# Inverting the first chunk's 32x32 blocks on TensorE instead of on VectorE, in a fused DeltaNet and SwiGLU kernel

## The chip, the cores and the metric

One core of one Trainium2 chip. The metric is the device time of one execution in microseconds (us). Stretches and waits are read from the one profiled execution of each kernel; that of the kernel before took 882.93 us. In the profile PE is TensorE, PEld its weight loads, DVE VectorE, ACT ScalarE, POOL GpSimd.

## The reference

Two stages, all in float32; the FFN weights arrive as 64-bit floats and are narrowed on the chip.

```python
# q, k, v: (4, 8, 768, 48); beta: (4, 8, 768)
k_n = k / (np.linalg.norm(k, axis=-1, keepdims=True) + 1e-06)
for t in range(S):
    kt, vt, bt = (k_n[:, :, t], v[:, :, t], beta[:, :, t, None])
    y[:, :, t] = np.einsum('bhd,bhde->bhe', q[:, :, t], state)
    v_old = np.einsum('bhde,bhd->bhe', state, kt)
    state = state + bt[:, :, :, None] * np.einsum('bhd,bhe->bhde', kt, vt - v_old)
# y is reshaped to 3072 tokens of 384; then, with rms-normed tokens xn:
g = xn @ w_gate                          # 384 x 1536
silu = g * (1.0 / (1.0 + np.exp(-g)))
return silu * (xn @ w_val) @ w_out       # 1536 x 384
```

## The kernel before

It cuts the 768 time steps into six chunks of 128. Chunk c of batch element b (eight heads) is a "unit"; there are 24. Inside a chunk the loop over t becomes matrix products, once the inverse of a unit lower triangular 128x128 matrix per head is known. The kernel inverts only its four 32x32 diagonal blocks and gets the rest by products ("corner"). FFN tiles take two units (256 tokens) each, so a chunk feeds two FFN tiles.

For each chunk all 128 blocks (4 per head, 8 heads, 4 batch elements) are sent through DRAM (`gd`) so that each block lies on one partition (`gblk`), and 31 steps of substitution with two vector instructions each turn the identity into the inverses (`ttb`). They return through DRAM (`td`) to the layout of the products (`tt`). `ne` is the same, scaled by minus beta.

```python
    def invert(c, dt):
        nc.gpsimd.memset(ttb, 0.0)
        nc.gpsimd.memset(ttb.rearrange("p j i -> p (j i)")[:, 0 : W * W : W + 1], 1.0)
        yield dt
        for i in range(W - 1):
            # ... shapes ...
            nc.vector.scalar_tensor_tensor(
                out=tmp,
                in0=gblk[:, i, None, i + 1 :].to_broadcast(shape),
                scalar=nbeta[:, c, i : i + 1],
                in1=ttb[:, 0 : i + 1, i : i + 1].to_broadcast(shape),
                op0=ALU.mult, op1=ALU.mult,
            )
            to = ttb[:, 0 : i + 1, i + 1 :]
            nc.vector.tensor_tensor(out=to, in0=to, in1=tmp, op=ALU.add)
            yield dt
        if c == 0:
            stay_warm(13, ttb[:, 0:4].rearrange("p k j -> p (k j)"))
        td = dram.tile([128, W, W], FP32, name="td")
        nc.sync.dma_start(out=td, in_=ttb)
        # ... for c > 0 the same with -beta into nd; then 16 transfers td -> tt
```

`stay_warm(n)` issues n matmuls nobody reads, to keep TensorE's clock up. The FFN weights come in tiles of 768 columns, and five vector instructions convert each; `convert(n)` places n of these steps in order by hand, and `convert_rest` deals the others out over time.

```python
        if c == 0:                       # in recur(), units 0 and 1 of chunk 0
            corner(0, None)
            corner(1, None)
            convert(1)
            stay_warm(2)
            corner(None, 0)
            # ... inner, outer, with convert() and stay_warm() between ...
            transpose_y(1, scale(*ys.pop(1)))
            convert(4)
            yield                        # from here on the FFN runs beside it
            # ... units 2 and 3 ...
```

All that follows is interleaved by a plan: a list of generators, each with a start time in steps, and each `yield dt` puts its generator dt steps later. One step is a group of FFN matmuls. The plan fixes the order in which each engine meets its instructions on the chip.

```python
    CYC = 3 * FT * B // 2
    first = recur(0, 1.2)
    # ...
    at(0, convert_rest(0.6))
    at(1, first)
    for c in range(1, NCH):
        t0 = CYC * c
        for b in range(B):
            at((8 if c == 1 else t0 - 76) + 4.5 * b, prepare(B * c + b))
        at(35 if c == 1 else t0 - 49, invert(c, 0.62))
        at(*((57, recur(c, 0.7)) if c == 1 else (t0 - 25, recur(c, 1.2))))
```

## Time and profile before

| what | value |
|---|---|
| time, median of 3 runs | 876.22 us (876.17 to 877.04) |
| profiled execution | 881.2 us |
| first FFN matmul (p_gv) | 89.8 us |
| chunk 0's FFN done (equal point, worked out in the prediction) | 233 us |
| from there to the end | 648 us |

The page of the kernel before cuts its span into 40 slices of 22 us. Each digit is a busy share in tenths; PEclk is the granted TensorE clock in tenths of full speed:

```profile
PE   6428789898999999999999999999999999999998
DVE  7594758986253491333491333491343491221100
PEclk9556889999999999999999999999999999999999
DMA  7722625402231103122103122113121113000000
```

The first four slices are the prologue. The "4" and "2" of PE, second and third, stand above the "5" and "9" of DVE: TensorE waits while VectorE substitutes, and its clock drops to 5. From the eleventh slice on PE is full. The rows of the page's table of groups for the two things that the change exchanges (line, engine, operation, tiles, shapes, count; then busy us, mean ns of one; then the idle time before them):

```profile
L443 DVE SCALAR_TENSOR_TENSOR tmp<-gblk,nbeta,ttb 128x31 f32<-128x31 f32 (+15 forms) x186 | 74.7, 402 | 13.9 <-DMA gblk<-gd 8.2
L452 DVE TENSOR_TENSOR ttb<-ttb,tmp 128x31 f32<-128x31 f32 (+15 forms) x186 | 63.6, 342 | 6.4
L793 PE MATMUL p_gv<-xt,wg_sb 128*128 128x256 f32 x864 | 218.3, 388 | 0.6 <-DVE xt L764 0.6
```

186 is six chunks of 31 steps, so a chunk's substitution costs (74.7 + 63.6)/6 = 23 us of VectorE. Only chunk 0's is exposed, since nothing else can run then.

### The profile page before, as it was taken

The numbers are of one execution on the slowest core, as the hardware profiler recorded it, in microseconds if no ns is written. First come the engines' busy times: TensorE is split into PE (matmuls) and PEld (weight loads), VectorE is DVE, ScalarE is ACT, GpSimd is POOL, SyncE is SP. The second block draws the span as 40 slices with busy tenths as digits, with TensorE's granted clock in tenths as the row PEclk, the third lists the DMA queues.
The fourth block names the chain that finished last, engine by engine and source line by source line (L and its number), as shares of the span: only waits on it lengthen the run. The fifth ranks groups of instructions, "written<-read, shape, count | busy, mean of one in ns | idle before, by whom it ended". The sixth has DMA issues, their size and how long they took to land.

```text
span 881.2 us, 20181 instructions
## 1 busy us (share of the span) xinstructions
PE 820.0 (93%) x8608; PEld 636.0 (72%) x8608; DVE 410.2 (47%) x1032; ACT 253.6 (29%) x651; POOL 95.3 (11%) x125
## 2 busy tenths in 40 slices
PE   6428789898999999999999999999999999999998
PEld 5327567676787777787777787777777777777776
DVE  7594758986253491333491333491343491221100
ACT  5503335511434312234212234212234212220101
POOL 3001132300041000131000131000130000000000
PEclk9556889999999999999999999999999999999999
DMA  7722625402231103122103122113121113000000
GB/s 187 184 72 51 181 82 157 130 5 84 48 74 34 42 19 85 38 65 39 37 34 69 38 65 40 36 42 61 38 56 22 37 43 61 2 19 1 19 0 19
DMA packets 147849, 51.05 MB, mean 58 GB/s; under 512 B 140176, under 2 KB 143248, under 8 KB 147760
## 3 DMA queue, kind: packets, MB, share of 16 engines
q1 hardware_dynamic: 123840, 35.34, 17.1%
q0 software_dynamic: 1872, 10.22, 3.5%
q10 hardware_dynamic: 22048, 4.20, 2.4%
q8 instruction: 68, 1.11, 0.5%
q14 instruction: 21, 0.17, 0.1%
HBM read 36.11 MB, written 13.63 MB: 56 GB/s over the span
## 4 chain that ended last, share of the span: by engine, by line
PE 78%; DVE 14%; DMA 2%; issue 2%; SPq 1%; ACT 1%; POOL 1%; ACTq 0%; DVEq 0%; POOLq 0%
PE p_gv L793 38%; PE p_o L780 19%; DVE tmp L443 5%; DVE ttb L452 5%; PE p_g L329 3%; PE p_y L567 2%; PE p_z L623 2%; PE p_k L605 2%; PE p_t L313 2%; PE p_y L605 2%; PE p_v L511 2%; PE p_x L641 2%; PE p_w L518 1%; PE p_z L632 1%; DVE h_f L804 1%
## 5 line engine op out<-in xcount | busy, mean ns | idle before, releaser
L780 PE MATMUL p_o<-wo_sb,h_f 128*128 128x384 f32 x576 | 217.5, 502 | 9.9 <-DVE h_f L804 9.8
L793 PE MATMUL p_gv<-xt,wg_sb 128*128 128x256 f32 x864 | 218.3, 388 | 0.6 <-DVE xt L764 0.6
L793 PE MATMUL p_gv<-xt,wv_sb 128*128 128x256 f32 x864 | 215.8, 386 | 0.0
L793 PEld LDWEIGHTS p_gv<-xt,wg_sb 128*128 128x128 f32 x864 | 161.6, 193 | 40.8 <-issue 1.7
L793 PEld LDWEIGHTS p_gv<-xt,wv_sb 128*128 128x128 f32 x864 | 161.5, 191 | 24.8 <-issue 2.5
L804 DVE TENSOR_TENSOR h_f<-sil,p_gv 128x256 f32<-128x256 f32 x144 | 60.2, 418 | 248.3 <-ACT sil L802 248.1
L802 ACT ACTIVATE sil<-p_gv 128x256 f32<-128x256 f32 x144 | 55.2, 383 | 332.0 <-PE p_gv L793 305.8
L780 PEld LDWEIGHTS p_o<-wo_sb,h_f 128*128 128x128 f32 x576 | 105.2, 192 | 62.8 <-DVE h_f L804 15.1
L443 DVE SCALAR_TENSOR_TENSOR tmp<-gblk,nbeta,ttb 128x31 f32<-128x31 f32 (+15 forms) x186 | 74.7, 402 | 13.9 <-DMA gblk<-gd 8.2
L452 DVE TENSOR_TENSOR ttb<-ttb,tmp 128x31 f32<-128x31 f32 (+15 forms) x186 | 63.6, 342 | 6.4
L343 DVE TENSOR_TENSOR gp<-p_g,mask 64x128 f32<-64x128 f32 (+1 forms) x160 | 37.6, 276 | 35.2 <-ACT gp L339 30.9
L293 POOL TENSOR_TENSOR knrm<-ksum,half 128x8 f32<-128x8 f32 x24 | 40.2, 1679 | 61.0 <-DVE ksum L292 60.9
L749 POOL TENSOR_SCALAR ms<-ms 128x1 f32<-128x1 f32 x24 | 6.5, 273 | 287.3 <-ACT y L741 287.0
L318 ACT COPY kqt<-p_t 128x512 f32<-128x512 f32 x48 | 28.0, 584 | 29.6 <-PE p_t L313 29.0
L548 ACT COPY vs<-p_v 32x256 f32<-32x256 f32 x48 | 17.4, 363 | 53.1 <-PE p_v L511 30.6
L623 PEld LDWEIGHTS p_z<-v_raw,tt 64*64 64x64 f32 x768 | 25.8, 142 | 9.4 <-issue 7.2
L435 POOL MEMSET ttb<- 128x1024 f32 x6 | 5.7, 955 | 240.5 <-DMA td<-ttb 189.1
L329 PE MATMUL p_g<-kqt 64*64 64x192 f32 x640 | 31.2, 330 | 0.0
L641 PE MATMUL p_x<-tt,gp 64*64 64x64 f32 x384 | 29.8, 233 | 0.1
L623 PE MATMUL p_z<-v_raw,tt 64*64 64x48 f32 x768 | 28.8, 227 | 0.0
L511 PEld LDWEIGHTS p_v<-tt,gp 32*32 32x32 f32 x768 | 17.6, 108 | 15.5 <-issue 11.1
L641 PEld LDWEIGHTS p_x<-tt,gp 64*64 64x64 f32 x384 | 26.4, 145 | 2.2 <-issue 1.6
(97 smaller groups left out, 803.7 us busy)
## 6 DMA issues: line engine op xcount, KB each, us to landing
kpad<-in_k_dram SPq DMA_DIRECT2D x24, 192.0 KB, 2.9
qpad<-in_q_dram SPq DMA_DIRECT2D x24, 192.0 KB, 2.7
v_raw<-in_v_dram SPq DMA_DIRECT2D x24, 192.0 KB, 3.0
raw<-in_moe_w_out_dram POOLq DMA_DIRECT2D x6, 768.0 KB, 5.0
out_dram<-o_sb SPq DMA_DIRECT2D x24, 192.0 KB, 1.9
gblk<-gd SPq DMA_DIRECT2D x6, 512.0 KB, 3.3
td<-ttb SPq DMA_DIRECT2D x6, 512.0 KB, 2.6
tt<-td SPq DMA_DIRECT2D x96, 32.0 KB, 2.2
```

Source lines behind the costliest of these rows:

```text
L293: nc.gpsimd.tensor_tensor(out=knrm, in0=ksum, in1=half, op=ALU.pow)
L329: nc.tensor.matmul(to, pair[d, K1 if i else K0], pair[d, places], skip_group_check=True)
L343: nc.vector.tensor_tensor(out=to[p, :, place], in0=p_g[p, :, place], in1=mask[p, i, None].to_broadcast([p.stop, 2, HC]), op=ALU.mult,)
L443: nc.vector.scalar_tensor_tensor(out=tmp, in0=gblk[:, i, None, i + 1 :].to_broadcast(shape), scalar=nbeta[:, c, i : i + 1], in1=ttb[:, 0 : ...
L452: nc.vector.tensor_tensor(out=to, in0=to, in1=tmp, op=ALU.add)
L605: nc.tensor.matmul(p_o[p, 2 * j : 2 * j + 2].rearrange("p h d -> p (h d)"), kq[:, j, place], st[:, j], start=(alone or j == 0), stop=alone ...
L623: nc.tensor.matmul(p_zs[b_z][p, h], tt[b_z][p, h], r[p, h], start=(h == 0), stop=(p is lo), skip_group_check=True,)
L641: nc.tensor.matmul(p_x[lo, h], gp[b_x][hi, h, HC * K0 : HC * (K0 + 1)], tt[b_x][hi, h], skip_group_check=True,)
L780: nc.tensor.matmul(p_o[i], h_f[:, i * C : (i + 1) * C], wo_sb[:, f], start=(f == f0), stop=(f == f1 - 1),)
L793: nc.tensor.matmul(p_gv[:, i], w_sb[:, t, f * 128 : (f + 1) * 128], xt[:, t], start=(t == 0), stop=(t == KT - 1),)
L802: nc.scalar.activation(out=sil, in_=p_gv[:, 0], func=ACTF.Silu)
L804: nc.vector.tensor_tensor(out=h_f, in0=sil, in1=p_gv[:, 1], op=ALU.mult)
```

## The change

The intent: get to the first FFN matmul sooner. Chunk 0's blocks are inverted where they lie, by block products on TensorE: no trip to DRAM, no 31 steps. A block is split into its eight 4x4 diagonal sub-blocks and the rest. The inner part A has A^4 = 0, so I-A has the inverse (I+A)(I+A^2); with that, the rest is some X with X^8 = 0, and I-X has the inverse (I+X)(I+X^2)(I+X^4). With the products at both ends this makes six steps of one or two rounds, each round 32 products of 32x32 blocks per unit: 320 matmuls, after 32 products of keys. Chunks 1 to 5 keep the substitution.

```diff
+    def blocks(n):
+        tiles = [(h, slice(W * a, W * (a + 1))) for h in range(H) for a in range(NBLK)]
+
+        def times(to, left, right, start=True):
+            for h, wa in tiles:
+                nc.tensor.matmul(
+                    to[wa, h],
+                    left[wa, h],
+                    right[wa, h].rearrange("p s w -> p (s w)")
+                    if len(right.shape) == 4
+                    else right[wa, h],
+                    start=start, stop=True, skip_group_check=True,
+                )
+        # ... p_d: 32 products of keys; weigh: times beta and a mask ...
+        p = ps_one()
+        plus(p, over_h(eye))
+        times(p, b_t, a_t, start=False)
+        nc.scalar.copy(a_t, p)
+        yield
+        # ... four more steps ...
+        p = ps_two()
+        times(p[:, :, 0], rx[:, :, 1], rx[:, :, 0])
+        times(p[:, :, 1], rx[:, :, 0], rx[:, :, 1])
+        # ... tt[n] and ne from p
```

The second part: a weight tile is now two k slices by 384 columns, so that the first FFN columns need three tiles instead of six, and fewer conversion steps (19 instead of 31) stand ahead of the FFN.

```diff
-WT = 768
+WT = 384
-    wg_sb = const.tile([128, KT, DFF], FP32, name="wg_sb")
-    wv_sb = const.tile([128, KT, DFF], FP32, name="wv_sb")
+    wgv_sb = const.tile([128, 2 * KT, DFF], FP32, name="wgv_sb")
...
-            raw = bits.tile([128, WT], I64, name="raw", bufs=3)
+            raw = bits.tile([128, 2, WT], I64, name="raw", bufs=3)
```

The order is new, too. `go(n)` is one step of unit n's blocks; those of units 2 and 3 partly fall behind the FFN's start (the `yield`), and all fill matmuls but the first 14 are gone:

```diff
+    def load_beta():
+        # ... four transfers into nbeta
+        nc.vector.tensor_scalar(
+            out=nbeta, in0=nbeta, scalar1=-1.0, scalar2=None, op0=ALU.mult
+        )
...
+            go(0)
+            query(1)
+            go(1)
+            transpose(3, kpad[3], K0)
             corner(0, None)
             corner(1, None)
+            go(2)
             convert(1)
-            stay_warm(2)
             corner(None, 0)
             corner(None, 1)
+            go(3)
...
             yield
+            go(3)
+            yield dt
+            go(2)
+            yield dt
+            key(2)
...
             inner(2, None, 3)
+            load_k(B)
+            load_beta()
+            mask_queries(2)
```

To make room for them, the plan sets chunk 1 and all later chunks 11 steps later (chunk 1's preparation 15). The paces of chunk 0's recurrence (1.2 to 0.8 steps) and of `convert_rest` (0.6 to 0.4) change too.

```diff
-        t0 = CYC * c
+        t0 = CYC * c + 11
-            at((8 if c == 1 else t0 - 76) + 4.5 * b, prepare(B * c + b))
-        at(35 if c == 1 else t0 - 49, invert(c, 0.62))
-        at(*((57, recur(c, 0.7)) if c == 1 else (t0 - 25, recur(c, 1.2))))
+            at((23 if c == 1 else t0 - 76) + 4.5 * b, prepare(B * c + b))
+        at(47 if c == 1 else t0 - 49, invert(c, 0.62))
+        at(*((68.5, recur(c, 0.7)) if c == 1 else (t0 - 25, recur(c, 1.2))))
```

## The prediction

> **What bounds the kernel now.** I read the page's 40 slices first, then busy time by stretches, the chain of work in the first 240 us, who PE waited for, and last the stretches around two stalls that the waits call "issue". The stretches give engine busy time, then granted TensorE clock, DMA share and GB/s:
>
> ```profile
> 0.00:240.00 240.00, 185.72 (x2356) 145.03 (x2358) 165.68 (x364) 85.10 (x194) 38.93 (x50) 0.84 0.41 107
> 240.00:860.00 620.00, 616.99 (x6196) 478.02 (x6190) 242.83 (x665) 166.04 (x451) 56.37 (x76) 1.00 0.17 40
> ```
>
> From 240 us on PE is busy 617 of 620 us at full clock: nothing but less PE work helps there, and the change takes none away. In the first 240 us, 54 us are idle and the clock averages 0.84. This is where all gain must come from. The chain there (shares of the whole span):
>
> ```profile
> by line: PE p_gv L793 18.5%; DVE tmp L443 9.5%; DVE ttb L452 8.3%; PE p_o L780 7.9%; issue 7.1%; PE p_z L623 2.4%; DMA tt<-td 2.2%; PE p_x L641 2.1%; DMA raw<-in_moe_w_gate_dram 2.0%; DMA gd<-gp 1.9%; PE p_w L518 1.9%; PE p_v L511 1.8%; PE
> ```
>
> The two DVE lines are the substitution, once for chunk 0 (about 31 to 57 us) and once for chunk 1 (180 to 210 us). In the timeline the first p_gv matmul of the FFN starts at **89.8 us**, after the blocks went out to DRAM (`gd`, landed near 31 us), 62 vector instructions, and the way back (`td`, `tt`, first use 66.6 us). From 66.6 to 89.8 us runs the recurrence of two units, half of it at clock 0.50. Waits of PE over the whole run:
>
> ```profile
> PE p_fill L183 <- DVE ttb L452: 14.2, 1, 14.2
> PE p_o L780 <- DVE h_f L804: 9.8, 7, 2.7
> PE p_g L402 <- ACT kqt L318: 8.6, 4, 2.9
> PE p_w L527 <- issue: 6.1, 2, 3.8
> ```
>
> The last row looks small and matters most for this change. The two stalls come in the only places where many 32x32 matmuls run without anything large between them:
>
> ```profile
> 66.60:68.30 1.70, 1.66 (x122) 1.52 (x123) 0.32 (x1) 0.39 (x2) 0.44 (x1) 0.51 0.64 84
> 68.30:70.60 2.30, 0.01 (x1) 0.01 (x2) 0.11 (x1) 0.34 (x1) 0.00 (x0) 0.50 0.86 315
> 99.68:100.85 1.17, 1.17 (x122) 1.17 (x121) 1.16 (x2) 0.46 (x2) 0.00 (x0) 1.00 0.92 360
> 100.85:104.86 4.01, 0.17 (x21) 0.06 (x9) 1.87 (x4) 0.36 (x1) 0.54 (x1) 0.91 0.51 110
> 104.86:115.00 10.14, 10.14 (x71) 7.74 (x71) 3.70 (x6) 3.59 (x8) 0.00 (x0) 0.53 0.18 71
> ```
>
> After some 60 matmuls (122 records: a matmul has two, and as many weight loads) PE stands still for 2.3 and 4.0 us, and after the longer one its clock is 0.53 for 10 us. The DMA view names the candidate:
>
> ```profile
> q8 instruction: 68, 1.11, 0.5%
> ```
>
> 68 packets of 16 KB are 17,408 instructions of 64 bytes; PE has 8608 matmul and 8608 weight-load records, 17,216 together. So q8 feeds PE, one packet lasts 256 instructions or **64 matmuls**, and its packets start at 67.75, 71.5 and 75.25 us, a distance of 3.75 us, with PE running again at 70.59.
>
> **What the Trainium skill says.** "Runtime: NRT & Kernel Launch", section "Instruction fetch mechanics", says that the sequencer fetches the next 16 KiB block of 256 instructions while it works on the current one, and that crossing a boundary is mostly hidden. The block size agrees with the trace; "mostly hidden" holds after 240 us and not in the two bursts above. "TensorE: Matmul & The Clock Gate", section "What's actually happening", says the clock falls to half after an idle window of about 3.4 us and rises after as much sustained work. The trace agrees roughly: 0.53 after the 4.0 us gap, 1.00 in the first 20 us with PE busy 67%, 0.61 in 20 to 30 us with PE busy 42%. "TensorEngine Tiling (Array Packing)", section "Key Properties", says that tiles work independently; with four diagonal 32x32 blocks in turn the trace has 59 matmuls in 1.17 us, 20 ns each, against 62 ns (32 in 1.98 us at clock 0.50, 16 in 0.99 at full) where only two blocks alternate.
>
> **The change, part by part.** I took instruction orders of both kernels and multiplied counts by durations of the trace before.
>
> Removed before the first FFN matmul: the 31 steps of substitution (62 DVE instructions, 23 us), `gd`, `gblk`, `td` and `tt` transfers of chunk 0, 27 of the fill matmuls, the transposes L527. The weight tiles also change: both kernels have 18 tiles of 768 columns' worth with 5 DVE steps (0.55+0.96+0.56+1.0+0.96 = 4.0 us), but the first FFN columns now need 3 tiles ready instead of 6, so 19 conversion steps stand ahead of the FFN instead of 31: about 9 us of DVE moved behind.
>
> Added per unit: 32 products p_d, 256 matmuls 32 wide and 64 matmuls 64 wide, four identity products. At 36, 20 and 30 ns and 0.42 us that is 1.2+5.1+1.9+1.7 = **9.9 us of PE**, some 40 us for four units. DVE gets about 3.6 us per unit, ACT nine copies of 0.37 or 0.59 us. With two units interleaved the six steps hide each other's copies.
>
> Start of the FFN. Summed by order, PE has 45 us of full-clock work between the first p_d (near 9.5 us) and the first p_gv. Walking the steps through PE, ACT and DVE with these durations gives the last block of units 0 and 1 near 37 us and the first p_gv at 56 us, if nothing else stands in the way. But these 45 us hold about 1220 matmuls, 1245 from the start, or 19.5 blocks of instructions. Two are there at the start; the first fetch begins at matmul 64, near 12 us; 17.5 fetches at 3.7 us (an estimate from the distance of 3.75 us above) are 65 us, so **12 + 65 = 77 us**. I take 75 (range 62 to 88): fetches are sometimes quicker than that, or hidden behind wider matmuls. Gain at this point 15 us, not the 34 that the steps alone would give.
>
> From there to the end of chunk 0's FFN. Before: 127.7 us (89.8 to 217.5) for 105 us of full-clock PE work, with four of 24 FFN column blocks (15.5 us) left; the equal point is 217.5+15.5 = 233 us. After: 136 us of PE work (93 FFN, 12 blocks of units 2 and 3, 31 scores, transposes and recurrence), since units 2 and 3 are now solved behind the FFN's start. DVE has 116 us in it. The 555 matmuls at its beginning are 29 us of work and 8.7 fetches, 32 us. With 8 to 10 us of other losses (before: 23, of which 4 the stall and some 6 the half clock) it is 148 us, and ends at 75+148 = 223 us.
>
> Then chunk 1's recurrence. The plan sets it and everything after it 11 steps later against the FFN; by the order PE has nothing of the FFN among its first 25 us of small matmuls. Before it lay among p_gv from 217.5 us and PE was 99.9% busy. I count 8 us lost to copies between the steps, less 2 for fewer switches between tile shapes: 6 us. From chunk 2 on both are the same.
>
> Sum: 233 - 223 - 6 = 4 us gained; optimistic at every estimate (start 62, middle 144) 21 us; pessimistic (88 and 155) a loss of 16. I shade the centre by some 4 us towards the optimistic side, because the start has the most doubtful estimate: **868 us**.
>
> **Rivals.** (a) Steps bind, fetch is hidden: FFN at 56 to 62 us, end 850 to 856. For it: after 240 us PE shows no such stall. Against it: there 64 matmuls take over 5 us (245 in the 20 us from 220), here some 2.2. (b) Half clock: with the fill matmuls gone and PE waiting on fetches and copies, the clock falls to 0.50 in the prologue; the small matmuls cost up to double, FFN at 80 to 88, end 875 to 885. For it: 0.50 from 30 to 60 us before. Against it: PE is then busier than 42%. (c) DVE becomes the bound behind the FFN's start, as 12 more conversion steps lie there and h_f stands behind them in order: 116 us in 148 is 78%, the same share as before (99.6 of 127.7), so I expect waits of p_o on h_f like the 9.8 us now, not a bound. (d) Uncovered recurrence of chunk 1 costs 15 us: then the time is that of before.
>
> **Range and chances.** Range 851 to 884, from the sums above with not all estimates off the same way. Faster by over 2% means under 859, a gain of 17.5 us, which needs rival (a) almost whole: 0.22. Slower by over 2% (over 894) needs (b) and (d) together: 0.05. Within 2%: 0.73.
>
> **What would show it.** The first p_gv near 75 us; PE stalls called "issue" between bursts of the block products, and packets of the instruction queue 3.5 to 4 us apart from 15 to 75 us; PE busy some 60% there. If the first p_gv comes before 64 us and those packets are 2 to 3 us apart, my fetch estimate is wrong and (a) holds. Chunk 0's FFN ending near 223 us, a stretch of some 32 us of recurrence without p_gv after it, and the same 660 us from there to the end as before would bear out the rest. A clock of 0.50 in the slices from 20 to 60 us speaks for (b).

## The result, and the profile after

The changed kernel is correct and slower. Its median is 927.69 us (926.32 to 932.21, four runs) against 876.63 us of the kernel before on the same chip (876.17 to 877.57, four runs). The ratio is **1.059** (95% interval 1.056 to 1.062). A ratio here is the mean time of one kernel's fast runs over that of the other's of the same rounds, so it is not quite the ratio of the medians quoted.

The page after:

```profile
span 930.4 us, 25271 instructions
PE   7778896889889999999999999999999999999998
DVE  6425448933923438424349133366143383121110
PEclk7877999989977999999999999999999999999999
q8 instruction: 88, 1.44, 0.6%
L511 DVE SCALAR_TENSOR_TENSOR tmp<-gblk,nbeta,ttb 128x31 f32<-128x31 f32 (+15 forms) x155 | 62.2, 401 | 10.0 <-DMA gblk<-gd 5.3
```

The substitution of chunk 0 is gone (155 = 5 x 31), and VectorE's full third slice ("9" before) is now a "2". PE is busier in the prologue than it was, and yet the prologue takes as long. There is also something new: PE's clock is at 7 in the twelfth and thirteenth slices, 256 to 302 us, where PE was at full clock before. The instruction queue q8 has 88 packets instead of 68.

Two marks cut both profiled executions into comparable stretches:

| stretch | before | after | difference | predicted |
|---|---|---|---|---|
| start to first p_gv | 89.8 | 88.7 | -1 | -15 |
| to the end of chunk 0's FFN | 143 | 172.5 | +29 | +5 |
| from there to the end | 648 | 669 | +21 | +6 |
| sum | 881 | 930 | +49 | -4 |

The sum differs by 49 us, the medians by 51. The end after is read from the last p_o matmuls of chunk 0's FFN, which finish at 261.2 us. Busy times by stretches (stretch, length, then busy time and records of PE, PEld, DVE, ACT, POOL, then granted clock, DMA share, GB/s), first of the kernel before:

```profile
10.00:89.80 79.80, 42.87 (x799) 36.21 (x799) 55.19 (x117) 29.24 (x61) 7.87 (x10) 0.66 0.45 113
89.80:233.00 143.20, 129.94 (x1349) 97.35 (x1350) 102.13 (x217) 49.49 (x121) 24.85 (x28) 0.93 0.37 102
```

and of the changed kernel:

```profile
10.00:88.70 78.70, 60.85 (x2417) 51.14 (x2415) 33.69 (x70) 28.24 (x64) 10.97 (x14) 0.72 0.25 69
88.70:261.20 172.50, 146.51 (x1978) 110.35 (x1978) 111.00 (x230) 56.73 (x137) 33.27 (x42) 0.95 0.31 88
261.20:305.80 44.60, 38.57 (x782) 35.42 (x781) 12.05 (x27) 12.57 (x32) 4.97 (x9) 0.73 0.31 62
```

In the first, PE stands idle for 18 us and is at 0.72 of its clock. In the second it is idle for 26 us, 13 more than before, and has 17 us more of work. The third is chunk 1's recurrence with no FFN matmul in it at all: chunk 0's FFN is used up, and chunk 1's needs what this recurrence makes. The longest waits of PE in the whole run:

```profile
PE p_b L557 <- issue: 15.8, 11, 2.3
PE p_o L1017 <- DVE h_f L1041: 15.6, 10, 3.1
PE p_y L718 <- DVE u L799: 5.8, 2, 5.0
```

p_b is the tile of the block products. Their timeline shows the bursts (start, length, then what ran; the bracket is the idle time before):

```profile
15.89 0.95 PE L557 MATMUL p_b<-wo_sb 32*32 32x32 f32 x51
18.52 0.42 PE L557 MATMUL p_b<-wo_sb 32*32 32x32 f32 x13 [1.67 <-issue]
```

The packets of the instruction queue start (to the half microsecond below) at 15.5, 19.5, 23.5, 27.5, 31.5, 34.5 us and so on to 86.5 us: 19 packets, 3.94 us apart on average, right up to the first p_gv.

### The profile page after: what moved, and what is told of

It reads as the page before. It is cut to its first block, busy times and chain, and to the rows that moved or that the text cites. A ratio compares the mean times of both kernels' runs of the same rounds, so it can differ in the third digit from the quotient of the medians.

```text
span 930.4 us, 25271 instructions
## 1 busy us (share of the span) xinstructions
PE 870.8 (94%) x11146; PEld 681.3 (73%) x11146; DVE 399.6 (43%) x1000; ACT 264.4 (28%) x684; POOL 108.8 (12%) x149
## 4 chain that ended last, share of the span: by engine, by line
PE 78%; DVE 13%; issue 4%; DMA 2%; ACT 1%; POOL 1%; SPq 1%; ACTq 0%; DVEq 0%; POOLq 0%
PE p_gv L1030 34%; PE p_o L1017 16%; DVE tmp L511 4%; PE p_b L557 4%; DVE ttb L520 3%; PE p_g L398 3%; PE p_t L382 2%; PE p_y L718 2%; PE p_z L774 2%; PE p_k L756 2%; PE p_x L792 2%; PE p_v L681 2%; PE p_y L756 2%; PE p_z L783 1%; PE p_w L688 1%
## 5 line engine op out<-in xcount | busy, mean ns | idle before, releaser
L1030 PE MATMUL p_gv<-xt,wgv_sb 128*128 128x256 f32 x1728 | 413.5, 386 | 0.7 <-DVE xt L1001 0.7
L1030 PEld LDWEIGHTS p_gv<-xt,wgv_sb 128*128 128x128 f32 x1728 | 322.0, 191 | 64.7 <-issue 3.7
L1017 PE MATMUL p_o<-wo_sb,h_f 128*128 128x384 f32 x576 | 217.5, 501 | 15.6 <-DVE h_f L1041 15.6
L511 DVE SCALAR_TENSOR_TENSOR tmp<-gblk,nbeta,ttb 128x31 f32<-128x31 f32 (+15 forms) x155 | 62.2, 401 | 10.0 <-DMA gblk<-gd 5.3
L520 DVE TENSOR_TENSOR ttb<-ttb,tmp 128x31 f32<-128x31 f32 (+15 forms) x155 | 53.0, 342 | 4.9
L358 POOL TENSOR_TENSOR knrm<-ksum,half 128x8 f32<-128x8 f32 x24 | 41.0, 1709 | 79.7 <-DVE ksum L357 75.1
L774 PEld LDWEIGHTS p_z<-v_raw,tt 64*64 64x64 f32 x768 | 28.3, 148 | 9.6 <-issue 6.6
L792 PE MATMUL p_x<-tt,gp 64*64 64x64 f32 x384 | 32.3, 241 | 1.8 <-ACT tt L701 1.8
L774 PE MATMUL p_z<-v_raw,tt 64*64 64x48 f32 x768 | 31.8, 235 | 1.3 <-issue 0.8
L718 PE MATMUL p_y<-u,gp 128*64 128x48 f32 x768 | 27.5, 227 | 5.8 <-DVE u L799 5.8
L718 PEld LDWEIGHTS p_y<-u,gp 128*64 128x64 f32 x768 | 26.3, 144 | 6.4 <-issue 5.3
```

The lines of the kernel that those rows point to most:

```text
L358: nc.gpsimd.tensor_tensor(out=knrm, in0=ksum, in1=half, op=ALU.pow)
L511: nc.vector.scalar_tensor_tensor(out=tmp, in0=gblk[:, i, None, i + 1 :].to_broadcast(shape), scalar=nbeta[:, c, i : i + 1], in1=ttb[:, 0 : ...
L718: nc.tensor.matmul(p_y[p, h], gp[b_y][:, h, HC * place : HC * (place + 1)], u[:, h], start=(c == 0 and h == 0), stop=True, skip_group_chec ...
L774: nc.tensor.matmul(p_zs[b_z][p, h], tt[b_z][p, h], r[p, h], start=(h == 0), stop=(p is lo), skip_group_check=True,)
L792: nc.tensor.matmul(p_x[lo, h], gp[b_x][hi, h, HC * K0 : HC * (K0 + 1)], tt[b_x][hi, h], skip_group_check=True,)
L1017: nc.tensor.matmul(p_o[i], h_f[:, i * C : (i + 1) * C], wo_sb[:, f], start=(f == f0), stop=(f == f1 - 1),)
```

## The experiments

Theory: **(1)** the prologue is bound by instruction fetch, 64 small matmuls per packet and some 4 us per packet, whatever the products cost; **(2)** the 11 steps of delay in the plan strip chunk 1's recurrence of its FFN cover, so it runs alone, at half clock; **(3)** VectorE's order (conversions and the wait for `nbeta` ahead of what the FFN needs) makes the idle time between. Rivals: the six steps' chain of copies binds the prologue and not the fetch; the weight tiles are at fault; the low clock is the cause and not a companion. The experiments ran in four calls, on chips 3 and 7, with medians of the kernel before between 879.08 and 881.47 us instead of 876.63; so they are compared by ratio to the kernel before of their own call. The changed kernel itself was not run again, so ratios that differ from its 1.059 by less than about half a per cent are not told apart. The first p_gv comes from one execution each: the change, e_plan and e_warm share one prologue and have it at 88.7, 86.8 and 88.4 us, so 2 us there mean nothing.

| run | what | ratio to before | 95% interval | first p_gv us | chunk 1's first p_v us |
|---|---|---|---|---|---|
| (before) | | 1 | | 89.8 | 217.4 |
| (the change) | | 1.059 | 1.056 to 1.062 | 88.7 | 262.6 |
| e_pair | 2 heads per block product (wrong result) | 1.030 | 1.024 to 1.036 | 75.1 | 242.5 |
| e_quad | 4 heads per block product (wrong result) | 1.026 | 1.020 to 1.032 | 62.1 | 228.3 |
| e_plan | the 11 steps undone | 1.041 | 1.036 to 1.046 | 86.8 | 247.6 |
| e_tiles | before + weight tiles | 0.996 | 0.990 to 1.001 | 86.0 | 205.6 |
| e_warm | clock kept up in chunk 1 | 1.055 | 1.050 to 1.060 | 88.4 | 263.5 |
| e_beta | `nbeta` negated later | 1.051 | 1.047 to 1.055 | 88.3 | 258.5 |
| e_qpb | quad + plan + beta (wrong result) | 1.004 | 0.998 to 1.009 | 66.8 | 216.3 |
| e_tiles2 | before + tiles, converted later | 1.003 | 0.999 to 1.008 | 86.4 | 213.7 |
| e_conv | change + 12 conversions earlier | 1.054 | 1.050 to 1.058 | 93.0 | 262.2 |
| e_pbc | plan + beta + conv | 1.035 | 1.032 to 1.038 | 90.9 | 242.3 |
| e_qpbc | quad + plan + beta + conv (wrong result) | 0.998 | 0.994 to 1.003 | 67.8 | 207.1 |
| e_tiles3b | before + tiles, converted earlier | 0.989 | 0.985 to 0.993 | 90.7 | 207.6 |

### Fewer, wider block products: e_pair and e_quad

One matmul takes the columns of two (or four) heads, with the left block of the first. The result is wrong on purpose (relative error 0.11 and 0.14), but the steps, copies and bytes stay; only matmuls and weight loads become fewer, and each wider.

```diff
             for h, wa in tiles:
+                if h % 4:                      # 2 in e_pair
+                    continue
+                hs = slice(h, h + 4)
                 nc.tensor.matmul(
-                    to[wa, h],
+                    to[wa, hs],
                     left[wa, h],
-                    ... right[wa, h]
+                    ... right[wa, hs]
```

> The changed kernel, but each block product takes two heads in one matmul (one stationary block, 64 or 128 streamed columns instead of 32 or 64): the result is wrong on purpose, the columns streamed and the chain of steps are the same, and 640 of the 1280 block matmuls fall away, 10 instruction packets. Theory of instruction fetch: the first FFN matmul moves from 88.7 us to 65 to 75 us, the time falls by 20 to 37 us, to 890 to 907 us. Rival (the chain of steps, the array's own time, or the half clock sets the start): less than 6 us change, 921 us or more.

> The same with four heads in one matmul: 960 of 1280 block matmuls fall away, 15 packets. Fetch: the first FFN matmul at 55 to 68 us, the time 30 to 50 us below the changed kernel, 878 to 897 us, with less gained by the second halving than by the first since then the steps bind. Rival: less than 6 us change.

Measured: the first p_gv comes at 75.1 and 62.1 us instead of 88.7, with 78 and 73 instruction packets in all instead of 88. The prologue of e_quad, and the stretch behind it:

```profile
10.00:62.10 52.10, 46.61 (x1169) 34.77 (x1167) 33.38 (x70) 27.54 (x64) 10.95 (x14) 0.84 0.37 101
62.10:227.00 164.90, 144.29 (x1306) 106.19 (x1306) 111.30 (x231) 56.16 (x137) 33.64 (x42) 0.94 0.32 92
```

From 10 us to the first p_gv, PE is idle for 5.5 us instead of 17.9 and has a clock of 0.84 instead of 0.72. The chain of steps and copies is whole in this kernel, so that rival falls: the number of matmuls bound the prologue. 26.6 us came back at the first p_gv, though the waits called "issue" before it in the changed kernel sum to only 13.4 us. The rest is busy time, 46.6 us instead of 60.9. Busy time times clock is some 39 us instead of 44 (an estimate from these lines), so the rest is partly work saved (about 5 us at full clock) and partly the higher clock. The second line shows what did not come back: the way from the first p_gv to the end of chunk 0's FFN still takes 165 us.

Since fewer matmuls also mean fewer weight loads, this pair of runs cannot quite tell fetch from the array's own work. The probes below do.

### The disputed cost by itself: e_probe_n and e_probe_w

In the kernel before, PE stands idle while chunk 0 is substituted. There, 192 matmuls of 32x32 by 32 columns were put in, or 48 with 128 columns: the same columns streamed, a quarter of the instructions.

```diff
+            if i == 25:
+                for r in range(192):           # 48 in e_probe_w
+                    x = slice(W * (r % NBLK), W * (r % NBLK + 1))
+                    nc.tensor.matmul(
+                        p_fill[0][x, 0:32], ident[x, x], ident[x, 0:32], skip_group_check=True
+                    )                          # 0:128 in e_probe_w
```

> The kernel before with 192 extra 32x32 matmuls of 32 columns (four diagonal tiles in turn, fp32, result unused) in the stretch from 43 to 57 us, where PE only waits for DVE and DMA is 20% busy. Theory of instruction fetch: bursts of about 64 matmuls with pauses between, one packet of the instruction queue per burst, 3.5 to 4 us apart, 10 to 13 us in all, 55 to 65 ns each. Rival (a fixed issue cost of each small matmul): an even row without pauses, the same spacing from first to last, 20 to 35 ns each, 4 to 7 us in all.

> The same columns in 48 extra matmuls of 128 columns. Theory: less than one packet, no pause of over 1.5 us, 4 to 7 us in all. If the array's own time bound the narrow ones, both take the same time.

One look each (880.65 and 880.36 us, both correct, no interval). The added matmuls in the timeline; first the narrow ones, of which each makes two records:

```profile
42.58 1.84 PE L878 MATMUL p_fill<-ident 32*32 32x32 f32 x153
46.25 1.56 PE L878 MATMUL p_fill<-ident 32*32 32x32 f32 x128 [1.83 <-issue]
49.98 1.61 PE L878 MATMUL p_fill<-ident 32*32 32x32 f32 x103 [2.17 <-issue]
```

and the wide ones:

```profile
41.23 4.65 PE L878 MATMUL p_fill<-ident 32*32 32x128 f32 x96
```

The narrow ones run 64 matmuls (128 records) in 1.56 us and then stop until the next packet. The packets start at 43.5, 47.25 and 51.0 us: 3.75 us for 64 matmuls, of which 1.6 is work. The wide ones, with as many columns in all, run without a pause in 4.65 us and need one packet, at 42.25 us. They also load weights a quarter as often, but a burst that ends at 64 matmuls, stops, and goes on when the next packet has come is not a cost of weight loads: the pause belongs to the number of instructions. What the probes do not settle is the end of the prologue: from 60 to 80 us of the changed kernel PE is busy for 17.9 of 20 us at a clock of 0.51, and there fetch and the half clock cannot be told apart.

### The plan's 11 steps: e_plan

```diff
-        t0 = CYC * c + 11
+        t0 = CYC * c
-            at((23 if c == 1 else t0 - 76) + 4.5 * b, prepare(B * c + b))
+            at((12 if c == 1 else t0 - 76) + 4.5 * b, prepare(B * c + b))
-        at(47 if c == 1 else t0 - 49, invert(c, 0.62))
-        at(*((68.5, recur(c, 0.7)) if c == 1 else (t0 - 25, recur(c, 1.2))))
+        at(36 if c == 1 else t0 - 49, invert(c, 0.62))
+        at(*((57.5, recur(c, 0.7)) if c == 1 else (t0 - 25, recur(c, 1.2))))
```

> The changed kernel with the plan's shift of 11 steps taken back (chunk 1's preparation at 12, its inversion at 36, its recurrence at 57.5, every later chunk 11 steps earlier), so that chunk 1's recurrence lies among FFN matmuls again, as before. Theory that the uncovered recurrence costs (44.6 us for 25 us of work): the time falls by 10 to 20 us, to 908 to 918 us. Rival (PE then waits in its order for DVE's inversion of chunk 1, which is no earlier): within 5 us of 927.7 us.

Measured: 1.041, which is 1.8 points less, correct. Its stretches:

```profile
86.80:247.60 160.80, 133.57 (x1914) 100.31 (x1915) 109.56 (x225) 55.17 (x133) 35.68 (x42) 0.92 0.34 95
247.60:300.00 52.40, 49.93 (x932) 40.24 (x933) 17.63 (x43) 16.57 (x42) 10.60 (x14) 1.00 0.29 57
```

Chunk 1's recurrence, from 247.6 us, now has FFN matmuls among it: PE is busy for 49.9 of 52.4 us at a clock of 1.00, against 38.6 of 44.6 at 0.73. So (2) holds: the delay, meant to make room, cost about 15 us (1.8% of 877 us). It could be taken out without another change.

### The half clock: e_warm

Eight fill matmuls go into each of the first three steps of chunk 1's recurrence.

```diff
+            if c == 1 and s < 0:
+                p_warm = ps_delta([128, 128], "p_warm")
+                for i in range(8):
+                    nc.tensor.matmul(p_warm, ident, ident, skip_group_check=True)
```

> The changed kernel with eight 128x128 fill matmuls ahead of each of the first three steps of chunk 1's recurrence, so that PE is busy while it waits for tt from DRAM. In the changed kernel that recurrence takes 44.6 us, at clock 0.50 from 266 to 288 us, for some 25 us of work. Theory (the gaps at its start drop the clock, and the half clock costs): clock near 1.00 there, the gap between FFN matmuls of 45.5 us falls to 28 to 36 us, the time by 8 to 16 us to 912 to 920 us. Rival (its chain of copies costs): the gap stays over 40 us and the time within 3 us of 927.7 us.

The same two stretches, first of the changed kernel, then of e_warm:

```profile
270.00:275.00 5.00, 5.00 (x87) 4.52 (x86) 0.56 (x1) 1.36 (x4) 0.00 (x0) 0.50 0.49 117
275.00:280.00 5.00, 5.00 (x75) 4.58 (x75) 1.10 (x2) 1.32 (x3) 0.00 (x0) 0.50 0.23 50
```

```profile
270.00:275.00 5.00, 4.93 (x133) 4.44 (x132) 0.56 (x1) 1.72 (x5) 0.00 (x0) 1.00 0.37 57
275.00:280.00 5.00, 5.00 (x145) 4.59 (x142) 1.66 (x3) 1.83 (x5) 0.00 (x0) 1.00 0.47 123
```

The fills bring the clock to 1.00, and PE gets through 278 records instead of 162 in the same ten us. From the end of the last p_o to the next p_gv it is 44.6 us in the changed kernel (261.2 to 305.8) and 38.4 us in e_warm (262.2 to 300.6); the 45.5 us of the expectation were read with another mark. Only 16 of the 24 fills lie in this gap, the other eight ran at 229 us among the FFN. The 16 are 4.6 us of work, of which some 2 us only fill waits for `tt` (3.6 us in the changed kernel, 1.6 in e_warm). So the recurrence alone would take some 34 to 36 us at full clock, and the half clock costs some 9 to 11 us there; this is an estimate from these numbers. The fills spend a good part of what they save. In the time itself 1.055 is not told apart from 1.059.

### VectorE's order: e_beta and e_conv

e_beta moves the negation of `nbeta`, which waits for its transfer, from `load_beta` to the start of chunk 1's substitution, out of the way of `u`, which stood behind it in order. e_conv puts twelve conversion steps back ahead of the FFN.

```diff
-        nc.vector.tensor_scalar(out=nbeta, in0=nbeta, scalar1=-1.0, ...)   # load_beta
+        if c == 1:                                                         # invert
+            nc.vector.tensor_scalar(out=nbeta, in0=nbeta, scalar1=-1.0, ...)
```

```diff
-            convert(3)
+            convert(9)
...
-            convert(1)
+            convert(7)
```

> The changed kernel with the negation of nbeta moved from just behind its transfer's issue to the start of chunk 1's inversion. Theory: the wait of p_y for u of 5.0 us goes (DVE stood in order behind the transfer of nbeta), and the time falls by 4 to 7 us. Rival (DVE's conversions take the place of this wait): less than 2 us.

> The changed kernel with 12 more conversion steps ahead of the FFN, placed where its DVE is idle (37.2 to 54.9 us), so 31 as in the kernel before. Theory (12 steps, some 9.5 us of DVE, were moved behind the FFN's start although it did not come earlier, and DVE bounds the stretch from there to chunk 1's recurrence): the first FFN matmul stays at 87 to 91 us, chunk 1's recurrence starts 5 to 10 us earlier than 261.2 us, the time falls by 5 to 10 us. Rival (PE's own work and fetches bound that stretch): less than 3 us.

The wait of VectorE in the changed kernel, and what PE still waited for `u` in e_beta, where it had been 5.8 us:

```profile
DVE nbeta L237 <- DMA nbeta<-in_beta_dram: 3.9, 1, 3.9
```

```profile
PE p_y L719 <- DVE u L800: 3.2, 2, 2.5
```

The wait shrinks by 2.6 us and does not go. The profiled execution is 4.3 us shorter, but that of the change was the slowest of its runs (span 930.4 us, the others 924.5 to 926.4, against 926.1 here), so this says nothing. The ratio, 1.051, lies 0.8 points under that of the change, but on another chip, where e_warm and e_conv, too, lie 0.4 and 0.5 under it. With e_conv PE waits 9.8 us for `h_f` between its first p_gv at 93.0 us and 262 us, instead of 12.6 us; but its first p_gv comes 4.3 us later, and chunk 1 starts at 262.2 us instead of 262.6. What was won behind the FFN's start had been paid ahead of it. My expectation of a gain is not borne out. So of (3) the waits are seen in the traces; that mending them wins time is not shown.

### Together: e_qpb, e_pbc and e_qpbc

> Four heads per block matmul (wrong result on purpose), the plan's shift taken back and the negation of nbeta moved, all three together. If the three costs are separate they add: 900.8 - 11.6 - 5 = 884 us (880 to 889). If they share a cause (a later stage has to wait for chunk 1's inversion on DVE anyway), the sum is less: 890 us or more.

> The changed kernel with three parts mended, result correct: the plan's shift taken back, the negation of nbeta moved, 12 conversion steps ahead of the FFN. If they add (11.6, 5 to 6, and 5 to 10 us): 900 to 907 us. If they share the wait for chunk 1's inversion: 908 to 915 us. Above 880 us in any case, since the instruction fetch stays.

> The same three and four heads per block matmul (wrong result on purpose): what is left of the change's loss when fetch, plan, nbeta and conversions are all mended. Theory: below the kernel before at last, 868 to 878 us, since the FFN starts near 67 us instead of 89.8 and DVE's 97% busy stretch behind it is relieved. Rival (the extra 15 us of PE work behind the FFN's start eats it): 880 us or more.

Quad takes 3.3 points off the loss of 5.9, plan 1.8, beta perhaps 0.8: 5.8 if they add (from the ratios before rounding). Measured together (e_qpb): 1.0035, so 5.5 points. They add within the intervals, and little is left. e_pbc has the plan and VectorE's order mended, with correct results, and still loses 3.5%; quad on top of it (e_qpbc) brings 3.7 points back, so that is the block products. The earlier conversions may be worth 0.5 points in e_qpbc (0.998 against 1.004), but those intervals overlap, and e_pbc shows no gain by them: this stays unclear.

What this shows about the idea: with the instructions cut to a quarter (and a wrong result), the first p_gv comes 23 us earlier than before, at 66.8 us, and the time is no better. Between there and chunk 1's recurrence:

```profile
66.80:216.30 149.50, 129.98 (x1242) 96.15 (x1243) 109.45 (x225) 55.01 (x133) 34.26 (x42) 0.92 0.37 102
```

against, in the kernel before,

```profile
89.80:217.50 127.70, 114.44 (x1003) 85.07 (x1005) 99.63 (x212) 43.50 (x105) 24.85 (x28) 0.92 0.38 108
```

22 us more, 15.5 of them PE work. By the order of instructions this is the blocks of units 2 and 3, and their scores and transposes, which the kernel before did beside VectorE's substitution, when PE had nothing else. They now stand behind the FFN's start, where PE is the bound. Chunk 1 starts at 216.3 instead of 217.5 us.

### The weight tiles alone: e_tiles, e_tiles2, e_tiles3b

The kernel before with the change's tiles alone; then with 19 conversion steps ahead of the FFN as in the change; then, the other way, with 37 and with the change's order of fetches.

```diff
-WT = 768                                # all three: with wgv_sb, todo, fetch, words of the change
+WT = 384
@@ e_tiles2
-            convert(1) ... convert(4)   # the 12 steps between corner and transpose_y
-    at(0, convert_rest(0.6))
+    at(0, convert_rest(0.4))
@@ e_tiles3b
-            convert((1, 2, 2, 5)[n])
+            convert((1, 2, 2, 9)[n])
-        convert(4)
+        convert(6)
-            if i > 1:
-                fetch()
+            fetch()
```

> The kernel before with the change of weight tiles alone (two k slices by 384 columns, 18 tiles as before, same number of conversion steps ahead of the FFN). If the tiles alone matter: more than 5 us either way from 876 us. My theory, that the block products and the plan made the loss: 871 to 881 us.

> The kernel before with the new weight tiles and with 19 conversion steps ahead of the FFN, as in the changed kernel, in place of 31 (the 12 steps among the first recurrence are moved behind). Theory that those steps delay the FFN's start: the first FFN matmul moves from 86.0 us to 76 to 82 us, the time to 866 to 873 us. Rival (the chain over PE and ACT sets it, or DVE gives it back later): within 3 us of 877 us.

> The kernel before with the new weight tiles and six more conversion steps ahead of the FFN (37 in place of 31), raw tiles fetched as in the changed kernel. Theory that steps ahead are free while DVE waits for DRAM: 868 to 875 us. Rival: 877 us or more.

The tiles are not at fault: 0.996, with 1 in the interval. Fewer conversions ahead of the FFN (e_tiles2) did not bring the first p_gv earlier, 86.4 us against 86.0: VectorE's conversions were not what it waited for. Chunk 1 started 8 us later (213.7 us against 205.6). I had thought of waits for `h_f`, but these sum to 7.2 us in both. PE is idle for 17.8 us from the first p_gv to chunk 1 in e_tiles2 and for 11.6 us in e_tiles, and one wait of p_g for `kqt` from ScalarE, 3.8 us at 161 us, is in e_tiles2 alone; why it came, and where the rest of the 8 us arises, is not settled. I had expected a gain, so I turned it round: e_tiles3b has six more steps ahead than the kernel before. PE's waits for `h_f`, from 60 us on, in e_tiles and in e_tiles3b:

```profile
PE p_o L782 <- DVE h_f L806: 7.2, 3, 2.7
```

```profile
PE p_o L781 <- DVE h_f L805: 3.7, 2, 2.7
```

e_tiles3b has a median of 871.07 us (869.00 to 874.63, six runs) against 881.47 us of the kernel before, 0.989 (0.985 to 0.993), and is correct. It is **faster than both kernels**, than the one before by 1.1% (clear of 1), and it has none of the block products. How much of this is the tiles, the fetch order or the conversions was not separated; its interval overlaps with that of e_tiles.

## Why the prediction was wrong

The mechanism it named first was right, and so were most of its counts; three terms of the sum were too small, all in one direction, and the range did not allow for that. The largest miss is the middle one: 24.5 us, mostly waits of PE behind the FFN's start.

**Start of the FFN: predicted 75 us, measured 88.7.** The step "12 + 65 = 77 us" is mis-sized, and the shading to 75 made it worse. The fetch-bound stretch starts at 15.5 us, not 12, as the first p_d matmul comes at 12.57 us and not near 9.5; and 18 intervals take 3.94 us each, 71 us, where 17.5 times 3.7 were set. That gives 86.5 us, and the first p_gv follows two us later. "Fetches are sometimes quicker than that" was true of single ones (3.4 us at best) and not of the mean. The stalls "issue" and the packets came as it said they would, but PE was busy 77% of the time from 10 us on, not "some 60%", at a mean clock of 0.72: part of the time that the prediction gave to waiting for fetches passed as busy time at a low clock.

**From there to the end of chunk 0's FFN: predicted 148 us, measured 172.5.** PE's work was right: 146.5 us busy at a mean clock of 0.95 is 139 us, against 136. The failed step is "8 to 10 us of other losses", with 3 more for fetches: PE was idle for 26 us, and the clock took 7 more. The first three waits of the changed kernel in this stretch:

```profile
PE p_o L1017 <- DVE h_f L1041: 12.6, 6, 3.1
PE p_y L718 <- DVE u L799: 5.8, 2, 5.0
PE p_b L557 <- issue: 5.2, 4, 2.2
```

and the first of the kernel before, from 89.8 to 233 us:

```profile
PE p_o L780 <- DVE h_f L804: 6.8, 3, 2.7
```

The wait for `u` stood partly behind that for `nbeta` (in e_beta 3.2 us were left). The prediction expected waits for `h_f` "like the 9.8 us now" by comparing VectorE's share of time, 78%; a mean share says nothing about what stands in front of what, in order. The `nbeta` line stood in the diff, and the prediction does not mention it.

**Chunk 1's recurrence: predicted 6 us, measured 21.** It rightly saw that PE has none of the FFN among its first "25 us of small matmuls", and expected some 33 us with the copies. By e_warm that stretch is some 34 to 36 us at full clock, so this was close; measured were 44.6 us, some 20 more than the 25 us of work instead of 8. The term "8 us lost to copies between the steps" left the clock out: after waits of 3.6 us for `tt` at its start it was at 0.50 from 265 to 289 us, which cost another 9 to 11 us. e_warm's fills kept it up; whether by closing the gaps or by being large matmuls, it does not tell. e_plan shows that the 11 steps are the reason why the recurrence lies bare. Why the clock stayed at 0.50 with PE fully busy from 270 to 285 us is open. (The last check, "the same 660 us", had no clear mark to start from; by the sums it would have been 648 + 6.)

**The rivals.** (a) is false as to the change, but e_quad, with the first p_gv at 62.1 us, fits its estimate of 56 to 62 us for the steps alone. (b) is partly true: the clock was 0.50 from 10 to 20 us and 0.51 from 60 to 80 us, and 0.83 between, and 88.7 us for the FFN's start is near its 80 to 88; but removing instructions brought the clock to 1.00 from 20 to 40 us in e_quad, so there the low clock followed from the number of instructions; for 60 to 80 us this is not shown. (c), VectorE standing in the way "in order", is true in part (waits for `h_f` of 12.6 us, 6.8 before). VectorE is busy for 111 of 172.5 us, no bound on average, but for 28.9 of the 30 us from 158 us, where almost half of these waits lie (5.9 us); the kernel before has such a stretch as well (37.4 of the 40 us from 140 us). (d) is true: some 20 us by the stretches, and e_plan brought about 15 back.

One reading was wrong without entering the sum: where two 32x32 blocks alternate, 16 matmuls at full clock took 0.69 us in the trace (217.41 us), 43 ns each, not 0.99 us and 62 ns; 62 ns is right at half clock.

**The range** runs from 851 to 884 us, though the sums (21 us gained to 16 lost, from 876) give 855 to 892: it was shifted to the fast side, as the centre was. Of its parts, the start fell just past the edge of what was allowed (88 us), and the middle far outside (144 to 155 us). The range took errors "not all off the same way". They had one thing in common: each missed gap on PE, be it of a fetch, a copy or VectorE's order, came with a clock under 1 in the same stretch (0.72, 0.95, 0.73), where the sums took PE's work at full clock, so the errors were not independent. The chance given to "slower", 0.05, was for (b) and (d) together; both came, at least in part.

Left open: whether a correct version with fewer instructions per block product would gain. None was built. e_qpb and e_qpbc suggest that even then the time would be about that of before.

## What to carry to other kernels

Count instructions, not only their durations: where matmuls are so small that 64 of them take less time than a packet of the instruction queue (here 3.75 to 3.94 us), the packets' distance is their price. Here the same steps in a quarter of the block products started the FFN at 62.1 us instead of 88.7. Ask of work that is to be taken off a waiting engine where it ends up: here TensorE's idle time was the cheapest place for it, and moving work from under VectorE's substitution to behind the start of the bound gave back what the earlier start had won. When a plan is shifted to make room, look for the place where the next stage loses its cover.

## What the Trainium skill lacked or had wrong

- "Runtime: NRT & Kernel Launch", section "Instruction fetch mechanics", calls crossing a 16 KiB boundary "mostly hidden". For dense small float32 matmuls it is not: in the probe 64 matmuls (four instructions each) ran in 1.56 us and the next waited 1.8 to 2.2 us, and in the changed kernel packets came 3.94 us apart for 71 us. The page gives no fetch rate; these runs show one block of 256 instructions per 3.75 to 3.94 us. It also gives TensorE room for 2048 instructions; no such lead was seen, as the probe ran 77 matmuls, about 306 instructions, before its first pause, although PE had waited 2.5 us just before. The section's other size, two blocks of 16 KiB (512 instructions), is not contradicted.
- "TensorE: Matmul & The Clock Gate", section "Wait — 56ns, not 53.3ns?", says that start-to-start never drops below about 25 ns, however small the matmul. The sentence leaves out matmuls on different 32x32 tiles, which a later part of the page treats: with such tiles in turn the trace of the kernel before has 122 records in 1.17 us, about 10 ns each, or 20 ns for a float32 matmul of two records.
- The same page, section "What's actually happening", has the clock at full after some 3.4 us of sustained work. In the changed kernel it stayed at 0.50 from 270 to 285 us while PE was busy for 15.0 of 15 us. A PE that the profile counts as busy is not enough for the clock; the runs do not show what is.
- No page says what waiting for instructions costs beside the waits themselves. In the changed kernel the waits called "issue" ahead of the first p_gv summed to 13.4 us, none over 2.4 us, and e_quad brought 26.6 us back, with the clock at 0.84 instead of 0.72.
